# A planned attention and gated feed-forward kernel on one core: q put in token order at evacuation, eight weight tiles loaded in 512-column runs, and a new order table

## The chip, the cores and the metric

The kernel runs on one core of a Trainium2 chip. The metric is device time in microseconds (us) from one launch, the median of several runs. The five engines that matter are TensorE (PE in the profile, its weight loads PEld), VectorE (DVE), ScalarE (ACT), GpSimd (POOL) and SyncE (SP, which here only issues DMAs). ACT issues four of the loads too. Each engine takes its instructions strictly in the order in which the program gives them; engines wait for each other through semaphores.

## The reference, cut to what matters

```python
# q, k, v: (8, 8, 576, 64); chunks of 64 tokens; 72 chunks of 8 heads each
scores = (q_c @ k_c.T) / 8                    # 64 x 64 in each chunk and head
attn = exp(scores - max) / (sum + 1e-9)
x = (attn @ v_c), heads put side by side      # 4608 x 512
out = ((x @ w_a) * (x @ w_b)) @ w_out         # 512 -> 1536 -> 512
```

All inputs and the output are float32. The kernel computes in bfloat16 with float32 accumulation.

## The kernel before, in words

**Tiling.** The 4608 tokens are cut into 9 blocks (K) of 512 tokens, each of two units (u) of 256 tokens, each of four chunks. The 1536 inner columns are 12 tiles (ft) of 128. Attention is done unit by unit: q and k are loaded as float32 (`f32`), cast to bfloat16 (`qkb`), turned so that the head dimension lies on the partitions (`qkT`), multiplied into scores, exponentiated on ACT (`E`), summed and multiplied by v on PE; ACT takes ln and exp(-x) of the sums (`inv`), and DVE multiplies the two into `xT`, the feed-forward's input. Block 0 is done in four pairs of heads (`load_pair` to `values_pair`), so that it can begin before all of q and k is there. Units 2 and 3 (`TWO_UNITS`) are loaded with two neighbouring tokens in a row of 512 bytes and turned by PE (`cast_two`, `turn_pe`); all later units are turned by a transposing DMA (`turn_dma`).

**Feed-forward.** In blocks 0 and 1 each tile ft takes two chains of four matmuls (`ffn`: w_b into one PSUM bank, w_a into another). One engine copies the w_b bank to `bsb`, DVE multiplies it into the w_a bank and writes `AB`. From block 2 on the two products, and the product with w_out in all blocks, use seven instead of eight block products (Strassen's scheme in Winograd's form): sums and differences of the operands are made first (`side_sums`, `x_sums`, `out_sums`, `weight_sums`; DVE and POOL), and partial results are copied out of a PSUM bank (`keep_copy`) while the next product is added onto the same bank, so the next product into that bank waits for the copy (`side_group`, `out_seven`, `out_last`).

**Order.** Every instruction group is made by `op`, with the engines that may run it, a planned cost, and what it reads and writes. The order of all 1689 groups was found ahead of time and is written out in `ORDER_OF_ALL`: `e12` is group 12 on SP, `a` is PE, `b` ACT, `c` DVE, `d` POOL, digits after a colon are PSUM banks, and `f3` is a filler matmul on zeros into bank 3 that computes nothing. `follow` reads the table; the program is issued in that order. The costs given to `op` have no effect once the table stands. In the final loop a POOL group is made to wait for the DVE group last issued before it if that one is marked `fast` (works from SBUF to SBUF).

**Loads.** SP's queue takes the q pairs, v of block 0, weights, and the later units; the four k pairs are issued by ACT. A tile of w_a or w_b goes through a staging buffer (`wst`, eight of them, 512 KB each) and a cast into `WA` or `WB`. `load_w` brings 256 columns (two tiles, runs of 1 KB in memory) or 128 columns (one tile, runs of 512 bytes); `load_wo` brings two row tiles of w_out with all 512 columns (runs of 2 KB). SP's order up to the dense part of the program is: q pairs; v of block 0 mixed with tile 1 of w_b and w_a and k of unit 2; tiles 2 and 3; w_b of tiles 4 to 7; tile 0; q of unit 2; w_a of tiles 4 to 7; w_b of tiles 8 and 9; k and q of unit 3; and then the rest.

**Token order.** In block 0 a row of `f32` holds four neighbouring tokens, in units 2 and 3 two. After the turn, PSUM holds the tokens sorted by their place in the row. For k, the copy out of PSUM puts them in token order (`if x:` in `turn_pair` and `turn_pe`). For q it copies them as they stand, and the scores matmul reads q with a stride of one row of 128 (`scores_pair`, `chunk_of`).

Lines of the profile: L330 is `copy`, used by every cast and plain copy, so its groups are told apart by their tiles; L359 `load`; L481, L511 and L521 turn, scores and exponential of block 0; L612 and L649 turn of units 2 and 3 and scores of all later units; L762, L775 and L777 the two chains, the copy and the product of `ffn`; L847, L867, L881 and L885 product, kept copy, product of halves and addition of `side_group`; L914 and L917 its last steps; L1107 `out_sums`; L1151, L1164 and L1179 product, kept copy and addition of `out_seven`; L990 and L1013 those of the last block; L1446 the fillers.

Of the kernel before, what the change touches and what calls it, by code (L numbers as in the profile page):

```python
# [85 lines left out]
c132 e0 b1 e2 b3 e4 b5 c66 c75 c69 d78 d87 c84 e6 b7 c96 c93 f0 f1 f2 f3 f4 f5 f6 f7 f0 a67:0 c68 f1 f2 f3 f4  # L86
f5 f6 f7 f1 f2 f3 f4 f5 a88:1 a79:2 a85:3 e8 e10 e16 e11 e18 a70:4 b71 e14 e9 d102 d17 b86 f6 f7 a94:5 a97:6
b98 b95 c89 c80 a76:7 c77 a72:40 b74 b73 f3 f1 a99:31 b100 a90:65 b91 e134 c142 e15 a103:20 b105 b19 a81:47
e13 e12 b83 b82 f3 f6 f3 f6 f0 f3 a110:36 b101 a125:07 b92 a114:41 b111 b126 b112 b113 c115 b104 b106 a107:53
c109 c116 c108 f0 f0 f6 a143:0 c144 b127 a145:6 a118:24 b119 d117 f7 f3 a129:73 a122:21 b128 e35 c131 c130  # L90
b120 b121 c123 a169:5 b37 a170:4 c124 f0 f3 f0 a171 e32 d34 a179:0 b181 a180:3 d33 a175:7 b36 a176:2 e26 d28
a187:1 d27 e20 d21 b177 a172 a183:0 d22 c288 e38 e40 d39 b41 c296 c299 b173 c174 b185 a163:7 a164:5 a165 b167
e133 b146 e29 b31 e23 b25 b24 b30 c137 a140:4 c182 c141 c291 a191:0 b193 a166 c168 b189 c294 a138:3 b139 c178
a195:7 b197 e48 d50 a196:4 a184:6 e149 a203:5 a192:2 a215:01 a188:3 b216 b217 c287 d49 c186 b205 c250 c297
c157 a158:7 c198 e148 c152 e42 d43 d44 d302 a160:6 c161 a227:40 a153:1 b228 b154 b229 b230 c194 a155:5 c156
a207:6 c190 c159 b209 a199:4 a211:2 e135 e136 d147 a231:10 c300 e45 b46 b47 a235:53 b236 c290 c232 c233 a208:7
e51 b53 b52 b213 b237 a212:6 c214 d254 d255 e151 d303 c298 c210 a321:1 a200:5 b201 c202 a322:0 a309:2 a204:3
d289 c292 a354:64 e150 b162 a358:75 b311 c206 c260 b323 c324 d301 d304 d256 b356 b355 b357 c359 c360 a310:2
a317:1 a305:3 a325:4 a306:6 b307 c312 a313:0 a337:3 b315 a329:7 c308 b331 a341:0 a314:5 a342:2 a421:6 a318:7
e222 b319 c251 c316 c320 e62 b343 c344 a413:1 a333:0 a425:5 a326:7 e221 e60 b61 e218 b339 b423 e219 b224 b335  # L100
b327 c328 a338:2 a334:3 c336 e54 b55 a405:6 b407 c340 a417:0 a330:4 a426:7 b419 c332 a406:3 c408 d258 d295
d259 d252 d261 b415 e346 e56 e64 b65 e220 b225 a449:2 a409:6 b411 a410:0 c412 d293 a418:4 c420 a429:1 a422:3
a437:6 b439 a438:0 a430:4 b431 c432 e345 e348 e347 b352 d465 d351 d63 a414:6 c416 d57 c440 c238 c241 e58 b59
b427 b451 a445:1 a433:4 a446:6 a441:0 a442:5 c239 c424 b443 c242 c253 c245 c453 c240 c243 a262:2 a263 b264
e350 e223 b234 e349 c247 d466 c428 b447 c448 c444 a265:3 a450:0 c452 a268 a269 c244 c249 c246 e226 a362:71
c257 c461 a266 b270 a273 a434:6 c469 c248 b435 b363 c436 b364 b361 e353 a382:54 b384 b383 a374:07 b376 b375
c467 d457 d468 c267 a274 a271:1 a272 b275 c276 b377 a394:46 b395 a378:57 c380 e385 b396 e388 b397 a398:30 a277
a280 a281 e366 c379 c400 c399 a475:4 a531:7 a477:6 e369 e365 e367 b371 d462 c471 a278 a593:5 a540:0 c472 d474
e368 b476 b478 a538 c532 a533:3 c534 c473 e386 d391 e389 e390 e387 b279 b372 b539 a536 b537 e482 e481 c282
e480 c454 a541:2 a575:7 a542 b543 c544 a545 b546 e370 a591:3 a573:1 a552 b553 c547 d455 c470 a554 c535 d459  # L110
a556 a600:4 c557 b574 d392 d458 d548 a558 a596 c559 c592 b576 a598 a609:0 c594 b597 a602 e486 a549:2 e479 e373
d491 b599 a605 a601:3 a550 b606 a561:5 a615 b603 a613 c604 a617 c607 c608 b551 b610 b614 b401 c618 a619 c616
d463 a562 a402:14 a564 a631 d381 c555 a611:7 c620 d464 b403 b404 a494:61 b632 a565 a626:3 b612 a633 a637
a628:4 c563 e483 e484 e485 d492 c627 c629 d621 c560 c595 d630 e508 e510 e505 e393 a502:53 b495 e283 b496 b497
a498:61 c499 c500 c460 b566 a569 a570 c589 d456 b638 b634 a640 a635:4 b503 b504 a520:56 a524:31 e286 e511 b571
a652 c639 a577 a656 b521 b522 b523 c525 c526 c646 c644 b641 e514 e507 e506 b517 e667 e489 a636:5 a648:6 a578
c642 d645 d647 a567:3 a654 a650:1 b653 e509 e512 b518 a568 a658 a705:0 c657 c655 c659 c643 d660 b651 b649 a710
a714:4 b711 e285 b579 a712 a716 a707:7 b713 d622 c706 b717 c572 a580 a581 a719 e493 a528:50 b529 c718 c708
b720 a726 b727 e666 b530 a715:2 a730 a747:7 c582 c624 c623 c709 c721 c731 e488 e668 d587 d672 a749:3 b748
a765:5 c766 a732 c733 a728 c729 a770 b771 e665 d671 d734 b750 a767:6 c768 c661 c662 d664 e519 a682:04 b683  # L120
e487 e490 d501 d588 d590 a674:52 b676 a774:1 a776 b777 a775:0 b675 a772 b773 a787 b788 b684 a723:6 c778 a791
c792 b677 a785:2 a779 a678:57 a694:41 b695 c679 b780 c781 b696 d722 a724 a735:5 a736 a783:4 a802:1 c680 d782
b725 e284 c737 b786 c803 a793 c794 b784 a789 a800:7 c801 e687 e516 e585 e515 e685 e513 d527 e686 d691 a805
a738 c790 a698:51 e583 b697 c700 c699 e673 a702:07 e688 e871 b806 a807 b808 a822:3 a811 d692 d625 c820 c818
d819 a814 a809:1 a810:5 b812 b815 c813 b823 c816 a739 a826 a828 a830 c831 b704 b740 b827 c829 a844 b845 d663
a824:7 a832 a743 a744 c795 a841:4 e669 e670 d681 d817 c833 b703 b825 a846 a878:12 a850 d769 a839:0 c840 e869
e586 e870 b875 b745 a751 a752 e872 d876 c763 c804 c821 b881 b880 b882 b851 e693 a879:52 a905:10 c834 d837 c908
b753 b883 a860 b861 a848:6 c852 c842 d843 d798 e899 e689 e690 d701 a741:5 a742 c746 a864 b847 a853 b854 a914:3
b915 b884 d761 e898 d903 d762 d835 e877 e896 c907 a849:0 c855 c865 a754 a944 a755 c756 a866 c867 a939:4 b945
a948:1 d796 d836 a950 c940 b951 c952 e897 d902 d764 a929:26 a906:50 b909 b932 a916:4 b917 a961 b910 b933 b962  # L130
a857:5 a858 a965 c966 a974:2 a862 c863 a1052:06 b911 a928:31 c930 c931 a946 b947 a885:7 a957:3 b958 b1055 c975
e1043 a941:1 c942 b859 a886 e584 c887 e757 e874 e873 a979 b980 b1054 b1056 a953 b954 a949:6 a985 b986 d797
a888 a889 c799 a976:2 c838 c992 c856 d993 c955 c943 d868 d994 e1072 a963 c964 a959:1 b890 b960 c977 a983:7
c987 b912 e1044 b1049 e1045 e1046 d1050 a984:0 a967 a893 a981 c968 c995 a891:4 a1000 a996:2 a1004 c1005 b982
a988 b989 c978 c990 c991 b997 b1001 a998:6 a894 b895 b999 c937 d956 a892 a1013:7 c1014 a1002 a1006 a1018 b1019
e1071 e901 a1020 a918 c1007 b1021 c969 c1003 c1008 d1009 a1015:3 c1016 e760 e759 a919 b920 a1024 b1025 e904
a1079:70 a1053:13 b1057 b1058 c913 a1022:5 c1026 c970 d971 c1081 c1082 d1017 a1034 a921 a922 c923 a1038 c1039
e1048 c1011 e900 b934 e758 e1073 e1051 a1107:13 a1080:70 b1035 b1110 c972 a1027 b1028 a1023:2 c1029 a1090:4
a1119:1 a1036 c1037 a1040 c1041 d1010 d935 c936 d938 b1111 a1230:53 b1084 b1083 b1085 b1091 c1120 a1106:07
c1109 c1108 a1088:6 b1089 a1031:2 a1032 a1124 a1122 b1233 a1117:1 b1125 a1131 e1223 a1126:3 a1059:7 a1060  # L140
b1232 b1123 b1033 a1062 a1127:0 b1132 c1118 a1128 b1129 a1063 b1064 a1065:5 a1135:1 a1067 d1030 c973 e1070
d1076 d1170 c1172 c1171 c1061 e1075 e1222 e925 e1074 b1112 c1042 c1130 a1143 c1133 a1145 a1139 e1224 b1136
a1157 a1141 c1144 b1158 c1146 e1047 b1086 a1068 c1115 c1173 a1152:7 c1153 b1069 a1137:3 a1154:0 b1138 c1155
d1134 c1012 a1066 c1113 a1163 b1164 a1159 b1140 b1160 c1142 b1234 a1092 a1093 a1174:7 a1161:0 c1165 a1166
e1221 b1227 b1175 a1176:6 a1162:4 a1182 d1077 e927 e926 b1094 c1087 e1078 a1095 c1183 d1228 e1229 a1196
a1191:2 a1178 b1167 c1168 a1184 b1177 d1156 c1147 d1121 a1193:0 c1185 b1197 a1202 a1198 b1199 e1249 e1098
e1251 e924 e1100 c1192 c1194 d1148 c1186 d1114 d1149 b1203 a1200:4 c1204 b1179 a1180 c1181 a1096 c1097 e1250
e1103 e1101 a1205 b1206 a1212 b1213 d1169 d1187 d1189 d1151 d1195 a1216 c1217 a1214 c1215 a1201:2 a1231:01
a1257:35 b1236 b1235 a1281:74 b1284 c1207 c1260 c1259 a1266:6 b1267 b1285 a1218 c1219 a1268:1 b1269 a1291:0
# [31 lines left out]
def kernel(  # L181
# [116 lines left out]
    NWS = 8  # L298
# [975 lines left out]
    for n in names:  # L1274
# [13 lines left out]
        elif c == "O":  # L1288
            load_wo(i)
# [208 lines left out]
```

## Time and profile before

| what | us |
|---|---|
| median of 3 runs (296.96 to 298.87) | 296.99 |
| the profiled execution's own time | 296.97 |
| its span, first to last instruction | 295.2 |
| PE busy in the span | 289.9 |
| DVE, ACT, POOL busy | 205.8, 200.6, 172.9 |
| the two hardware DMA queues' share of 16 engines (q1, q10) | 71.9% and 1.1% |

The profile counts an engine as busy from the start of an instruction to its end; neighbouring instructions of one engine overlap a little, so the busy time of a group can be more than the time it keeps the engine from the next. A group's row gives line, engine, operation, tiles written and read, shapes and count, then busy us and mean ns of one. The time beside the span (1.8 us) lies before the first and after the last instruction.

### The profile page before, as it was taken

The page shows a single profiled execution, that of the slowest core. Times are in us where ns is not written, and L with a number is a line of the kernel's source. Part 1 is how long each engine was busy: PE and PEld are TensorE (multiplying, and loading weights), DVE is VectorE, ACT ScalarE, POOL GpSimd, SP SyncE. Part 2 cuts the span into 40 slices and gives each one's busy share as a digit, 9 for nine tenths or more (in the row PEclk, how much of TensorE's full clock was granted, in tenths as well). Part 3 has the DMA queues.
Part 4 walks back from the last instruction along what each step waited for, and adds up shares of the span by engine and source line. Part 5 has one row for each costly group of instructions (what it writes and reads, how often), then busy time and mean ns, then how long its engine had stood idle before and what let it go on. Part 6 is the DMA issues. An engine that isn't in the chain of part 4 may idle for free.

```text
span 295.2 us, 8644 instructions
## 1 busy us (share of the span) xinstructions
PE 289.9 (98%) x3537; PEld 236.3 (80%) x3539; DVE 205.8 (70%) x390; ACT 200.6 (68%) x365; POOL 172.9 (59%) x167
## 2 busy tenths in 40 slices
PE   8989999999999999999999999999999999999995
PEld 3644558877888888888888888888888888888884
DVE  2445876477776688686768886679777776667783
ACT  1776797868958977969487686677866655455331
POOL 2242387933488365976985366269747469695510
PEclk9999999999999999999999999999999999999999
DMA  7999999999999999999999976088730110021016
GB/s 256 318 372 337 266 300 298 283 228 234 230 222 234 207 200 249 231 223 240 251 223 219 223 184 167 2 193 218 180 73 3 53 73 3 1 109 71 2 66 219
DMA packets 146423, 55.08 MB, mean 187 GB/s; under 512 B 126288, under 2 KB 140752, under 8 KB 146384
## 3 DMA queue, kind: packets, MB, share of 16 engines
q1 hardware_dynamic: 145152, 53.43, 71.9%
q10 hardware_dynamic: 1232, 1.11, 1.1%
q8 instruction: 27, 0.44, 0.6%
q14 instruction: 12, 0.10, 0.1%
HBM read 37.75 MB, written 9.44 MB: 160 GB/s over the span
## 4 chain that ended last, share of the span: by engine, by line
PE 96%; ACT 2%; DVE 1%; issue 0%; DVEq 0%
PE F L847 44%; PE F L1151 25%; PE F L762 14%; PE F L990 3%; PE F L1446 3%; PE F L649 2%; PE F L673 2%; PE F L659 2%; PE F L481 1%; PE F L511 1%; PE F L612 0%; DVE xT L576 0%; ACT E L521 0%; ACT inv L550 0%; ACT inv L548 0%
## 5 line engine op out<-in xcount | busy, mean ns | idle before, releaser
L867 ACT COPY part<-F 128x512 f32<-128x512 f32 x105 | 59.8, 591 | 40.0 <-PE F L847 27.3
L885 DVE TENSOR_TENSOR bsb<-F,part 128x512 bf16<-128x512 f32 x63 | 43.2, 687 | 24.2 <-PE F L847 14.8
L881 POOL TENSOR_TENSOR AB<-AB,bsb 128x512 bf16<-128x512 bf16 x35 | 40.7, 1169 | 19.5 <-DVE wst L807 6.6
L1107 POOL TENSOR_TENSOR wst<-AB 128x512 bf16<-128x512 bf16 x27 | 31.4, 1165 | 19.1 <-DVE AB L881 6.2
L847 PEld LDWEIGHTS <-WA 128*128 128x128 bf16 x336 | 32.7, 98 | 4.3 <-issue 0.5
L1151 PEld LDWEIGHTS <-wst 128*128 128x128 bf16 x336 | 32.6, 98 | 4.1 <-issue 0.2
L847 PEld LDWEIGHTS <-WB 128*128 128x128 bf16 x336 | 32.6, 98 | 4.1 <-issue 0.2
L885 DVE TENSOR_TENSOR AB<-F,part 128x512 bf16<-128x512 f32 x42 | 28.8, 685 | 8.3 <-PE F L847 4.7
L1151 PEld LDWEIGHTS <-AB 128*128 128x128 bf16 x288 | 27.9, 98 | 3.5 <-issue 0.2
L847 PEld LDWEIGHTS <-Ta 128*128 128x128 bf16 x252 | 24.2, 98 | 3.4 <-issue 0.5
L847 PEld LDWEIGHTS <-Tb 128*128 128x128 bf16 x252 | 24.2, 98 | 3.3 <-issue 0.2
L712 DVE TENSOR_TENSOR xT<-F,inv 128x512 bf16<-128x512 f32 x32 | 20.7, 684 | 7.9 <-ACT inv L697 4.7
L847 PE MATMUL F<-wst,Ta 128*128 128x256 bf16 x168 | 25.3, 273 | 0.0
L847 PE MATMUL F<-wst,Tb 128*128 128x256 bf16 x168 | 25.2, 273 | 0.0
L847 PE MATMUL F<-wst,WA 128*128 128x256 bf16 x168 | 25.0, 273 | 0.0
L777 DVE TENSOR_TENSOR AB<-F,bsb 128x256 bf16<-128x256 f32 (+1 forms) x34 | 17.2, 529 | 11.2 <-ACT bsb L775 5.8
L762 PE MATMUL F<-xT,WA 128*128 128x256 bf16 (+1 forms) x136 | 24.9, 317 | 0.0
L847 PE MATMUL F<-wst,WB 128*128 128x256 bf16 x168 | 24.9, 273 | 0.0
L762 PE MATMUL F<-xT,WB 128*128 128x256 bf16 (+1 forms) x136 | 24.4, 316 | 0.4 <-DVE xT L576 0.4
L1151 PE MATMUL F<-WO,AB 128*128 128x256 bf16 x192 | 24.6, 273 | 0.0
L847 PE MATMUL F<-xT,WB 128*128 128x256 bf16 x168 | 24.6, 273 | 0.0
L847 PE MATMUL F<-xT,WA 128*128 128x256 bf16 x168 | 24.6, 273 | 0.0
(127 smaller groups left out, 585.0 us busy)
## 6 DMA issues: line engine op xcount, KB each, us to landing
f<-in_q_dram SPq DMA_DIRECT2D x28, 256.0 KB, 4.2
f<-in_v_dram SPq DMA_DIRECT2D x28, 256.0 KB, 4.5
out_dram<-osb SPq DMA_DIRECT2D x28, 256.0 KB, 3.2
f<-in_k_dram SPq DMA_DIRECT2D x24, 256.0 KB, 4.4
wst<-in_moe_w_out_dram SPq DMA_DIRECT2D x6, 512.0 KB, 5.8
wst<-in_moe_w_a_dram SPq DMA_DIRECT2D x5, 512.0 KB, 5.8
wst<-in_moe_w_b_dram SPq DMA_DIRECT2D x5, 512.0 KB, 6.5
f<-in_v_dram SPq DMA_DIRECT2D x16, 128.0 KB, 4.3
```

The lines of the kernel that those rows point to most:

```text
L649: T.matmul(PS[j][cl * 64:cl * 64 + 64, c:c + 64], chunk_of(u, 1, m, j, 2 * g + cl), chunk_of(u, 0, m, j, 2 * g + cl), start=True, stop=True,)
L712: op("dve", c_dve(512), lambda e, cl=cl: V.tensor_tensor(out=x.rearrange("p m (g c t) -> p c g m t", g=2, c=2)[:, cl], in0=f_of(PA[cl]).re ...
L762: T.matmul(f_of(b)[:, 0:n].rearrange("p (u t) -> p u t", u=len(us)), w[ft][:, kt, :], x[:, us[0]:us[-1] + 1, kt, :], start=(kt == 0), stop ...
L777: op("dve", c_dve(n), lambda e: V.tensor_tensor(out=AB[K % 2][:, ft // 2, ft % 2, us[0] * 256:us[0] * 256 + n], in0=f_of(banks[1])[:, 0:n] ...
L847: T.matmul(f_of(bank)[:, q * 256:q * 256 + 256], lhs(2 * g + q, kt), rhs[:, kt, :], start=(first and q == 0 and kt == 0), stop=(q == 1 and ...
L867: op("act", c_act(512), lambda e: A.copy(out=pab[s][i], in_=f_of(bank)), r=[("ps", id(bank))], w=[("part", s, i)], ps=[bank], prio=-400, a ...
L881: op(("dve", "pool"), TIMES, lambda e: ENG[e].tensor_tensor(out=dst, in0=dst, in1=b, op=MULT), r=bk, w=key, prio=-300, fast=True)
L885: op("dve", c_dve(512), lambda e: V.tensor_tensor(out=dst, in0=two(f_of(bank)), in1=two(pab[s][i]), op=ADD), r=[("ps", id(bank)), ("part", ...
L990: T.matmul(f_of(bank)[:, 0:256], lhs[:, i, h], rhs[:, i, :], start=(first and i == 0), stop=(i == NP - 1), skip_group_check=True)
L1107: op(("dve", "pool"), TWO_IN, lambda e, i=i, x=x, y=y, o_=o_: ENG[e].tensor_tensor(out=SS[i][:, s], in0=x[:, s], in1=y[:, s], op=o_), r=ft ...
L1151: T.matmul(f_of(bank)[:, at:at + 256], lhs[:, i, tt * 128:tt * 128 + 128], rhs[:, i, :], start=(first and at == 0 and i == 0), stop=(i == ...
L1446: "fn": lambda e: T.matmul(F[at], zero[:, 0:128], zero, start=True, stop=True),
```

## The change

1. `turn_pair` and `turn_pe` now put q as well as k in token order when they copy out of PSUM; the scores matmuls of block 0 and of units 2 and 3 then read q as contiguous columns.
2. Tiles 4 to 11 of w_a and w_b come by a new `load_four`: four tiles at a time (512 columns, runs of 2 KB), in two halves of the contraction dimension, each half through one staging buffer and one cast of 128x1024. Eight loads as before; eight casts where there were sixteen.
3. The engines that a group may run on are widened: weight casts, w_out casts, pair casts, unit casts and v casts may go to POOL, ACT or DVE; plain copies out of PSUM (`bsb`, `part`, `wst`, `osb`) to ACT or DVE; the w_out sums to DVE or POOL.
4. A new `ORDER_OF_ALL` (1681 groups) with new engines, banks, load order and fillers.

How the groups lie in the two tables, by engine (ACT / DVE / POOL):

| groups | before | after |
|---|---|---|
| all but DMAs and PE (ACT with its four loads) | 369 / 389 / 161 | 300 / 458 / 153 |
| kept copies of `side_group` | 126 / 0 / 0 | 86 / 40 / 0 |
| kept copies of `out_seven` | 24 / 0 / 0 | 17 / 7 / 0 |
| `bsb` copies of `ffn`, 512 and 256 columns | 34 / 0 / 0 | 16 / 18 / 0 |
| casts of w_a and w_b | 12 / 0 / 12 | 4 / 7 / 5 |
| casts of later units' q and k | 11 / 0 / 17 | 18 / 0 / 10 |
| casts of v | 9 / 0 / 9 | 8 / 4 / 6 |
| pair casts of block 0 | 0 / 6 / 2 | 3 / 2 / 3 |
| fillers on PE | 39 | 25 |

The core of the diff, the table left out but for its first words:

```diff
 ORDER_OF_ALL = """
-c132 e0 b1 e2 b3 e4 b5 c66 c75 c69 d78 d87 c84 e6 b7 c96 c93 f0 f1 f2 f3 f4 f5 f6 f7 f0 a67:0 c68 f1 f2 f3 f4
...
+c124 e0 b1 e2 b3 e4 b5 e8 e6 b7 c61 e15 e11 e10 e9 b58 f0 f1 f2 f3 f4 f5 f6 f7 f0 f1 a59:0 b60 b67 a62:1 d70
...
-    ORDER = "P0 P1 P2 P3 V0 V1 w1 W3 W2 q2 k2 W1 w0 W5 v2 W4 O0 k3 O1 O2 q3 O4 O5 v3 O3"
+    ORDER = "P0 P1 P2 P3 V0 V1 w1 W1 w0 q2 k2 X1 v2 X2 O0 k3 O1 O2 q3 O4 O5 v3 O3"
...
+    def load_four(src, name, i):
+        dst = WA if name == "a" else WB
+        for half in range(2):
+            s = count["w"] % NWS
+            count["w"] += 1
+            load(
+                wst[s].rearrange("p (k c) -> p k c", k=2),
+                src[half * 256:half * 256 + 256, i * 512:i * 512 + 512].rearrange("(k r) c -> r k c", r=128),
+                ("wst", s), (256, 71),
+            )
+            def cast(e, s=s, half=half):
+                return copy(e, dst[:, 4 * i:4 * i + 4, 2 * half:2 * half + 2, :], wst[s].rearrange("p (k f c) -> p f k c", k=2, f=4))
+            op(("pool", "act", "dve"), (1.04, 1.05, 0.69), cast, r=[("wst", s)], w=[("w" + name, 4 * i + n) for n in range(4)],
+               prio=5 + 4 * i * 0.1, fast=True)
...
             dst = qkT[hu][:, 8 * x + 4 * mm:8 * x + 4 * mm + 4, :]
-            if x:
-
-                dst = dst.rearrange("p a b -> p (a b)").rearrange("p (t r) -> p t r", r=4)
-                t = t.rearrange("p r t -> p t r")
+            dst = dst.rearrange("p a b -> p (a b)").rearrange("p (t r) -> p t r", r=4)
+            t = t.rearrange("p r t -> p t r")
...
-            tq = qkT[hu][:, 4 * mm:4 * mm + 4, :].rearrange("p r t -> p t r")
+            tq = qkT[hu][:, 4 * mm:4 * mm + 4, :].rearrange("p a b -> p (a b)")
...
-                            tq[j * 64:j * 64 + 64, n * 16:n * 16 + 16, :],
+                            tq[j * 64:j * 64 + 64, n * 64:n * 64 + 64],
...
         if u in TWO:
-            if x:
-                return t[:, 2 * m + c // 2, (c % 2) * 64:(c % 2) * 64 + 64]
-            return t.rearrange("p (m r) t -> p m t r", r=2)[:, m, 32 * c:32 * c + 32, :]
+            return t[:, 2 * m + c // 2, (c % 2) * 64:(c % 2) * 64 + 64]
...
-                op("act", c_act(512), lambda e: A.copy(out=pab[s][i], in_=f_of(bank)), r=[("ps", id(bank))], w=[("part", s, i)],
+                op(("act", "dve"), (c_act(512), c_dve(512)), lambda e: copy(e, pab[s][i], f_of(bank)), r=[("ps", id(bank))], w=[("part", s, i)],
```

SP's order in the new table is: q pairs with one v load before the last; the rest of v of block 0; tile 1; tiles 2 and 3; w_b of tiles 4 to 7; tile 0; w_a of tiles 4 to 7; k of unit 2; w_b of tiles 8 to 11; q of unit 2; w_a of tiles 8 to 11; v of unit 2; k and q of unit 3; and then the rest.

More of the change, by code (lines that the diff above doesn't have):

```diff
@@ L91 @@
[L91 to L95, printed above, removed]
@@ L237 @@
     HOLD = ()
-    W_CASTS = {(x, n): ("pool",) if x == "b" else ("act",) for x in "ab" for n in range(2)}
-    O_CASTS = [("pool","act")]
+    W_CASTS = {(x, n): ("pool", "act", "dve") for x in "ab" for n in range(2)}
+    O_CASTS = [("pool", "act", "dve")]
     WHOLE = False
@@ L402, in load_w @@
             engs = W_CASTS[name, ft % 2]
-            op(engs, [{"pool": 0.62, "act": 0.62, "dve": 0.42}[x] for x in engs], cast, r=[("wst", s)], w=[("w" + name, ft)], prio=5 + ft * 0.1)
+            op(engs, [{"pool": 0.62, "act": 0.62, "dve": 0.42}[x] for x in engs], cast, r=[("wst", s)], w=[("w" + name, ft)], prio=5 + ft * 0.1, fast=True)
+    def load_four(src, name, i):
[12 more added lines that the diff above has]
+               prio=5 + 4 * i * 0.1, fast=True)
     def load_wo(i):
@@ L728, in post @@
                    r=[("ps", id(PS[j]))], w=[("E", u % 2, n, j) for n in range(2)], ps=[PS[j]], prio=prio)
[L730 removed]
+        return 0.285, lambda: mm_scores(u, [f_of(x) for x in PS]), t_keys(u), PS, [], post
     def slot(prio, *parts, fixed=False):
@@ L916, in four @@
                 else:
-                    op("act", c_act(512), lambda e: A.copy(out=dst, in_=two(f_of(X))), r=[("ps", id(X))], w=key, ps=[X], prio=-400)
+                    op(("act", "dve"), (c_act(512), c_dve(512)), lambda e: copy(e, dst, two(f_of(X))), r=[("ps", id(X))], w=key, ps=[X], prio=-400)
             def three():
@@ L1163, in keep_copy @@
         def keep_copy(bank, i):
-            op("act", c_act(512), lambda e: A.copy(out=pu[i], in_=f_of(bank)), r=[("ps", id(bank))], w=[("pu", i, 0), ("pu", i, 1)], ps=[bank], prio=prio - 250, after=staged(4))
+            op(("act", "dve"), (c_act(512), c_dve(512)), lambda e: copy(e, pu[i], f_of(bank)), r=[("ps", id(bank))], w=[("pu", i, 0), ("pu", i, 1)], ps=[bank], prio=prio - 250, after=staged(4))
         o = []
@@ L1222, in four @@
             dst, key = place(1, 0)
-            op("act", c_act(512), lambda e: A.copy(out=dst, in_=two(f_of(X))), r=[("ps", id(X))], w=key, ps=[X], prio=prio - 240)
+            op(("act", "dve"), (c_act(512), c_dve(512)), lambda e: copy(e, dst, two(f_of(X))), r=[("ps", id(X))], w=key, ps=[X], prio=prio - 240)
         def three():
```

205 lines of the change are left out of this document (105 added, 100 removed).

## The prediction

> **What bounds the kernel now.** First the page (busy shares, slices, chain), then the chain in order of time, then the table of stretches with cuts where the chain changes, then the waits of PE.
>
> ```profile
> PE 289.9 (98%) x3537; PEld 236.3 (80%) x3539; DVE 205.8 (70%) x390; ACT 200.6 (68%) x365; POOL 172.9 (59%) x167
> ...
> DMA  7999999999999999999999976088730110021016
> ...
> PE 96%; ACT 2%; DVE 1%; issue 0%; DVEq 0%
> ```
> ```profile
> 1.26 4.02 PE F L1446 x9
> 5.71 2.61 PE F L1446 x12
> ...
> 18.82 1.42 DVE xT L576 x4
> 20.27 7.50 PE F L762 x34
> ```
> ```profile
> 0.00:20.27 20.27, 18.02 (x225) 10.02 (x228) 8.74 (x22) 11.43 (x27) 5.80 (x13) 1.00 1.01 312
> 20.27:292.11 271.84, 271.83 (x3312) 226.33 (x3311) 196.64 (x367) 189.21 (x338) 167.07 (x154) 1.00 0.72 178
> 292.11:295.20 3.09, 0.00 (x0) 0.00 (x0) 0.42 (x1) 0.00 (x0) 0.00 (x0) 1.00 0.38 126
> ```
> ```profile
> PE F L1446 <- DVE zero L1256: 1.3, 1, 1.3
> PE F L1446 <- ACT part L548: 0.4, 1, 0.4
> PE F L762 <- DVE xT L576: 0.4, 1, 0.4
> ```
> Columns of the third view: stretch, length, then busy us and count of PE, PEld, DVE, ACT, POOL, then clock, DMA share and GB/s. From 20.27 PE works without a gap to 292.11; its last wait is for xT of block 0. So there are three terms: a front of 20.27, a dense part of 271.84, and a tail of 3.09. PE is busy in the front too, but much of that is the 39 fillers. The DMA row says what else may bind: the DMA engines are full to about 170 us. The profiled run took 296.97, as the median does (296.99); 1.77 of it lie outside the span.
>
> **The front.** It ends when xT of block 0 is whole, and that ends a run of ACT. In the timeline of before, ACT waits to 9.26 for the first turned heads (PE's turns stand behind DVE casts in its order), then makes 25 instructions in 9.92 us, to 19.18; xT's last part and the first matmul on it follow 1.09 later. In the new table the first two casts of q lie on ACT and its first copy of a turned head comes behind one PE group, so ACT can start as q lands, at 4.1 (DVE's first cast starts at 4.09, ended by that DMA). The new table has 26 ACT groups up to that point, about the same work: 4.1 + 9.9 + 1.1 = 15.1 if ACT never waits. It will wait: heads land until 8.5 (DVE's cast ended by k at 8.54) and v follows. I add 1.3: 16.4. Bounds: 15.1, and 18.0 if ACT waits 2.9 (over half of the 5.1 it waited for the first turn before). A second count agrees: up to the dense part PE has 14.6 us of work in the old table, fillers included, and 10.2 in the new one (matmul intervals of the trace); with the same 5.7 of gaps that is 15.9. The fourteen missing fillers (14 x 0.22 = 3.0) are themselves free: they filled waiting.
>
> **q in token order.** Copying q strided costs DVE 0.69 in place of 0.41 (the tile view of qkT gives DVE copies 413 to 692 ns, and the k copies are the long ones); ACT's take 580 to 616 either way. Of the new q copies DVE has three: 0.8 us of DVE, in the front or beside dense PE, inside the above. Gain: a unit's scores took 0.69 where q is strided (33.76 and 39.60) and 0.45 where not (68.22): 2 x 0.24 = 0.5 off the dense part. Block 0's four lie in the front's waits. Against it, eight turns of k of unit 2 move from the front into the dense part: 8 x 0.056 = 0.45. Dense part: 271.8.
>
> **Loads and weights.** Ahead of tiles 2 and 3 the new queue has 3.7 MB (heads, v, tile 1) in place of 4.2 (k of unit 2 too): 0.5 MB at the 382 GB/s of 15 to 20 us is 1.4. Before, POOL's cast of tile 3 starts at 19.07, ended by its DMA; now 17.7. Then 1.05 MB of w_b, 2.75: 20.4, and its second half's cast on DVE, 0.69 by the row of 128x1024 casts: 21.2. PE, dense from 16.4, has tile 1's second halves and tiles 3 and 2 first, 20 matmuls of 0.216: it comes at 20.7 and waits 0.5. Then 3.15 MB (tile 0, w_a, k of unit 2, the next w_b) at the 340 GB/s of 20 to 30 us: 29.7, cast 30.4; PE, with 40 matmuls and four turns, is there at 30.05: 0.35. Unit 3's q comes 3.15 MB after that (q and v of unit 2, w_a, k), at 310 GB/s, between the rates of 20 to 30 and 40 to 45 us: 39.9. ACT's cast (1.05) ends at 41.0, PE wants to turn it 23.6 us of work and 1.2 of waits after 16.4, at 41.2: no wait, or a few tenths; I count 0.2. The scores, sums and values of unit 2 stand closer together than before (0.86 us of matmuls between scores and sums where there were 1.31, with two exponentials of 0.61 between): 0.35. Together 1.4, bounds 0 and 2.8. The front and this are coupled: what PE is late at the start, it need not wait for weights.
>
> What a load in 2 KB runs costs, no row shows in this stretch. The w_out loads have that form: median 5.8 us to landing for 512 KB, as w_a's 1 KB runs (5.8; w_b's 6.5). Bounds: 1.37 us each (384 GB/s, seen at 18 to 20 us) and 1.86 (282 GB/s, 40 to 45 us, w_out among heads); I take w_a's, so nothing changes, as the landing rows are nearest.
>
> Later loads: ahead of unit 4's transposing DMA the new SP order has one half-load of v less; its DMA was issued at 61.98 and unit 4's scores began at 68.22. In the new table scores 4 come 1.0 later in PE's work; with the front 3.9 sooner and 1.4 given back they begin at 66.7, 1.5 sooner, and the half-load (256 KB at 282 GB/s) takes off 0.9: hidden, with 0.6 less to spare. Units 8 and later come 8 to 20 us later in PE's work: more cover than before.
>
> **Engines.** Eight casts fall away (16 x 0.62 give 8 x 0.69 to 1.05), and 77 PSUM copies go from ACT to DVE: 62 of 0.69 and 15 of 0.42. DVE: 205.8 + 48 = 254 busy (86%), ACT 200.6 - 33 = 168. No row shows a DVE copy of 512 float32 columns; nearest is its addition from PSUM, 687 (L885), which I take; ACT's copy is 591 (L867), and between these the difference is nothing to 0.1 a copy. PE gives way only if a bank's next product comes sooner than the copy: the closest in the old table had 0.87 of matmuls for ACT's 0.59 and did not stop PE, so a copy needs its own length plus 0.28, for DVE 0.97; the closest kept copy on DVE has 1.01. Nothing, while the copy finds DVE free. Back to back, DVE starts the next about 0.09 before the last ends (four xT parts of 0.41 in 1.42), so its true load is nearer 75%.
>
> Sum: 16.4 + 1.4 + 271.8 + 3.1 = 292.7, and 1.8 outside: **294.5**.
>
> **Rivals.**
> (1) The weights and heads bind: the front is sooner, but DMA is as full as before. With the eight new loads halfway to their upper bound (+0.25 each, 2.0, all of it waited for, as PE is then short of weights) it is 296.5; at the bound itself 298.4. For it: DMA at 9 through 170 us. Against: PE never waited for a load after 20 us.
> (2) Slower: DVE becomes the bound. Of the copies now on DVE, 14 have under 1.66 of matmuls to their bank's next use. One DVE instruction of 0.69 ahead of each costs 4.1 together (the shortfalls summed): 298.6; two cost 16 over 23 copies: 311. Between, nearer the first: 300. It decides once more than 2.5 is lost. For it: DVE 196.64 of 271.84 in the dense part becomes 244, 90%, and DVE already waits little. Against: the 75% above, and ACT's 42 copies with under 1.66 cost nothing before. GpSimd belongs to it: in before, DVE's L1107 additions take 601 ns after a POOL row and 430 otherwise, 0.17 more. [...]
> (3) The clock: with fewer fillers PE may fall back to the rate of its first fillers (0.43 each, nine in 4.02; later twelve in 2.61, 0.22). Dense work at half rate for as long as that first stretch loses 2: 296.5. Against: in 9.7 to 15 us two to five fillers at a time kept 0.22. [...]
>
> **How the numbers follow.** Forecast 0.57, its own range 292.7 (15.1 front, 0.9 given back) to 296.1 (18.0 front, 1.4 given back); rival 1 0.20, rival 2 0.18, rival 3 0.05. Range 292.7 to 299.5: it takes in rivals 1 and 3 and the lower part of 2. About 1% is what a measurement of this kernel can tell from no change: faster means under 294.0, somewhat under half of the forecast's cases, 0.25. Slower means over 300.0, half of rival 2 and a little unforeseen, 0.15. The rest, 0.60.
>
> **What would show it.** Right: L762 without a gap from about 16.4, later gaps of 0.3 to 0.5 at the first w_b tile of tiles 4 to 7 and between unit 2's scores and sums, L649 at 0.45 in every unit, 25 fillers. Rival 1: PE waits for L330 casts that a DMA ended, at 20 to 45 us. Rival 2: PE L847 and L1151 waiting for DVE part or wst L330. Rival 3: L762's chains at 0.43 a matmul. The forecast is wrong if the front ends after 18, or if gaps after 45 us add up to over 1.5 more than before.

## The result, and the profile after

The changed kernel takes 294.77 us (median of six runs, 293.80 to 295.83); beside it the kernel before takes 297.64. The ratio is 0.9898, with a 95% interval of 0.9867 to 0.9930. Measured again on another chip it is 0.9925 (0.9899 to 0.9950). So the change is worth about 0.9%, some 2.6 us. The profiled run took 294.79, with a span of 293.0 and 1.8 outside it, as before. A few executions were clearly slowed (one of twelve in the run called d1 below took 521.18 us, with TensorE at 0.71 of its clock), and every ratio here leaves them out.

The page of the changed kernel first: engines, DMA row, chain of waits by engine.

```profile
PE 285.8 (98%) x3525; PEld 233.3 (80%) x3525; DVE 246.2 (84%) x459; ACT 174.6 (60%) x296; POOL 169.5 (58%) x159
...
DMA  7999999899998899999959999931919200013025
...
PE 92%; DMA 4%; SPq 2%; ACT 1%; issue 0%; ACTq 0%; DVE 0%
```

The share of PE is as large as before (98%). DVE has risen from 205.8 to 246.2 us and ACT has fallen from 200.6 to 174.6. New is that 6% of the chain that ended last is now DMA and SP's queue: the chain starts with loads. Next the table of stretches, cut at the first matmul that needs all of xT and at PE's last matmul (stretch, length, busy us and count of PE, PEld, DVE, ACT, POOL, then clock, DMA share, GB/s).

```profile
0.00:16.54 16.54, 13.81 (x205) 7.00 (x206) 8.77 (x20) 11.42 (x28) 3.15 (x10) 1.00 0.93 273
16.54:289.90 273.36, 272.00 (x3321) 226.31 (x3319) 237.03 (x439) 163.16 (x269) 166.34 (x149) 1.00 0.74 183
289.90:293.00 3.10, 0.00 (x0) 0.00 (x0) 0.43 (x1) 0.00 (x0) 0.00 (x0) 1.00 0.44 148
```

The front ends at 16.54 where it ended at 20.27: 3.73 us gained. The long stretch has grown from 271.84 to 273.36, though PE's busy time in it is the same (272.00 and 271.83): PE now stands idle for 1.36 us in it. The tail is as it was. Why the front is shorter, ACT's rows show: first those of before, then those of the change (start, us, line, what it does, and in brackets how long ACT waited and for what).

```profile
9.26 2.05 ACT L330 COPY qkT<-F 128x512 bf16<-128x512 bf16 x4 [5.14 <-PE F L481]
...
18.55 0.63 ACT L550 ACTIVATE part<-part 128x512 f32<-128x512 f32 x1
```
```profile
4.13 0.62 ACT L329 CAST qkb<-f 128x512 bf16<-128x512 f32 x1
5.33 0.58 ACT L329 COPY qkT<-F 128x512 bf16<-128x512 bf16 x1 [0.58 <-PE F L498]
...
15.05 0.63 ACT L565 ACTIVATE part<-part 128x512 f32<-128x512 f32 x1
```

ACT gets its first turned heads 3.9 us sooner (5.33 for 9.26), and its last step for block 0 ends 3.5 us sooner (15.68 for 19.18). Where the 1.36 lies, the chain in order of time and PE's waits say (engine, tile, line; what it waited for; us in total, times, longest).

```profile
1.79 5.63 DMA f<-in_k_dram
12.61 6.63 DMA wst<-in_moe_w_a_dram
20.46 9.67 PE F L774 x44
```
```profile
PE F L774 <- ACT WA L329: 1.1, 1, 1.1
...
PE F L671 <- ACT E L739: 0.2, 1, 0.2
```

The chain runs through the load of w_a of tiles 2 and 3 (issued at 12.61, landed at 19.24). The timeline around it shows the wait (L774 is `ffn`, L329 `copy`: the changed kernel's line numbers).

```profile
17.43 1.89 PE L774 MATMUL F<-xT,WB 128*128 128x512 bf16 x8
...
19.27 1.14 ACT L329 CAST WA<-wst 128x512 bf16<-128x512 f32 x2 [1.48 <-DMA wst<-in_moe_w_a_dram]
...
20.46 0.39 PE L774 MATMUL F<-xT,WA 128*128 128x512 bf16 x1 [1.13 <-ACT WA L329]
```

PE has used up its eight matmuls on w_b by 19.3; ACT starts the casts of w_a at 19.27, as soon as the data is there, and PE goes on at 20.46. From there it never waits for more than 0.2 us.

### The profile page after: what moved, and what is told of

The parts are those of the page before. It is cut to its first block, busy times and chain, and to the rows that moved or that the text cites. A ratio compares the mean times of both kernels' runs of the same rounds, so it can differ in the third digit from the quotient of the medians.

```text
span 293.0 us, 8646 instructions
## 1 busy us (share of the span) xinstructions
PE 285.8 (98%) x3525; PEld 233.3 (80%) x3525; DVE 246.2 (84%) x459; ACT 174.6 (60%) x296; POOL 169.5 (58%) x159
## 4 chain that ended last, share of the span: by engine, by line
PE 92%; DMA 4%; SPq 2%; ACT 1%; issue 0%; ACTq 0%; DVE 0%
PE F L859 44%; PE F L1163 25%; PE F L774 13%; PE F L1002 3%; DMA wst<-in_moe_w_a_dram 2%; DMA f<-in_k_dram 2%; PE F L661 2%; PE F L685 2%; SPq L358 2%; PE F L671 2%; PE F L627 1%; ACT E L739 0%; ACTq L358 0%; ACT WA L329 0%; DVE f L1030 0%
## 5 line engine op out<-in xcount | busy, mean ns | idle before, releaser
L329 ACT COPY part<-F 128x512 f32<-128x512 f32 x71 | 41.0, 589 | 38.6 <-PE F L859 25.1
L893 POOL TENSOR_TENSOR AB<-AB,bsb 128x512 bf16<-128x512 bf16 x42 | 48.3, 1156 | 19.2 <-DVE wst L1119 6.3
L329 ACT COPY wst<-F 128x512 f32<-128x512 f32 (+1 forms) x35 | 20.0, 571 | 30.8 <-PE F L1163 13.9
L1119 POOL TENSOR_TENSOR wst<-AB 128x512 bf16<-128x512 bf16 x23 | 26.4, 1158 | 10.6 <-DVE AB L893 7.5
L329 DVE COPY part<-F 128x512 f32<-128x512 f32 x34 | 23.2, 686 | 3.3 <-PE F L859 1.7
L774 PE MATMUL F<-xT,WA 128*128 128x256 bf16 (+1 forms) x136 | 24.4, 317 | 1.1 <-ACT WA L329 1.1
L329 ACT CAST bsb<-F 128x512 bf16<-128x512 f32 (+1 forms) x31 | 16.1, 534 | 15.0 <-PE F L859 8.3
```

What stands on the lines that cost most here:

```text
L329: return A.copy(out=out, in_=in_) if e == "act" else ENG[e].tensor_copy(out=out, in_=in_)
L774: T.matmul(f_of(b)[:, 0:n].rearrange("p (u t) -> p u t", u=len(us)), w[ft][:, kt, :], x[:, us[0]:us[-1] + 1, kt, :], start=(kt == 0), stop ...
L893: op(("dve", "pool"), TIMES, lambda e: ENG[e].tensor_tensor(out=dst, in0=dst, in1=b, op=MULT), r=bk, w=key, prio=-300, fast=True)
L1119: op(("dve", "pool"), TWO_IN, lambda e, i=i, x=x, y=y, o_=o_: ENG[e].tensor_tensor(out=SS[i][:, s], in0=x[:, s], in1=y[:, s], op=o_), r=ft ...
```

## The experiments

**Theory:** the gain is the earlier front, which the new table's order brings; from about 17 us the landing of weights limits PE, so part of the gain goes back there; token order of q and the wider loads are each worth half a microsecond or less. **Rivals:** (A) token order of q makes the front shorter; (B) the 2 KB runs bring the gain; (C) the copies taken off ACT bring it.

One table for all kernels whose long stretch stays dense. "Front" ends at the first matmul that needs all of xT; "rest" goes to PE's last matmul; "idle" is rest less PE's busy time in it; then the landing of w_a of tiles 2 and 3, the GB/s from 11 to 15 us, the profile's span, and the ratio to before in the timed runs.

| kernel | front | rest | idle | w_a lands | GB/s | span | ratio (95%) |
|---|---|---|---|---|---|---|---|
| before | 20.27 | 271.84 | 0.01 | | 316 | 295.2 | 1 |
| the change | 16.54 | 273.36 | 1.36 | 19.24 | 254 | 293.0 | 0.9898 (0.9867 to 0.9930) |
| a0_again | 17.36 | 274.40 | 2.43 | 21.11 | 199 | 294.8 | 0.9925 (0.9899 to 0.9950) |
| e1_q_strided | 16.91 | 272.70 | 0.23 | 18.30 | 250 | 292.7 | 0.9919 (0.9901 to 0.9937) |
| e2_1kb_runs | 16.59 | 273.56 | 1.10 | 18.40 | 261 | 293.2 | 0.9933 (0.9911 to 0.9956) |
| e8_cast_on_dve | 16.87 | 274.17 | 1.96 | 18.24 | 259 | 294.1 | 0.9919 (0.9889 to 0.9948) |
| e4_late_turns | 18.36 | 272.36 | 0.26 | 18.90 | 241 | 293.8 | 0.9882 (0.9837 to 0.9928) |
| e3_k2_ahead | 18.43 | 272.42 | 0.31 | 19.94 | 285 | 293.9 | 0.9930 (0.9898 to 0.9963) |
| d1_tile1_among_v | 19.78 | 272.38 | 0.23 | 18.52 | 308 | 295.2 | 0.9926 (0.9889 to 0.9962) |
| d2_tile1_between | 19.39 | 271.88 | 0.23 | 18.65 | 211 | 294.3 | 0.9879 (0.9841 to 0.9916) |
| e7_no_fillers | 18.05 | 272.96 | 0.23 | 19.10 | 249 | 294.1 | 0.9872 (0.9830 to 0.9914) |
| b1_old_q_order | 20.59 | 272.82 | 0.72 | | 295 | 296.5 | 0.9982 (0.9945 to 1.0020) |

These runs were made on several chips (before took 297.4 us on one, 298.2 and 300.0 on others) and the intervals overlap, so neither the times nor the ratios rank the variants of the change. Each profile is one execution; what it shows of the terms is read below.

### The changed kernel again

No edit.

> The changed kernel once more, as the base for the runs beside it. Theory and rivals alike: about 294.8 us, a front of 16.7 us, one stretch near 19 us in which PE waits about 1.3 us for w_a of tiles 2 and 3, and PE dense from there. If the lump in the landing of that load (2.76 us where its neighbours take 1.3) is chance, the wait is missing here, and the time is up to 1.3 lower.

Measured: 295.14, ratio 0.9925. The wait is there, and longer:

```profile
PE F L774 <- ACT WA L329: 2.2, 1, 2.2
```

The load of w_a landed at 21.11, 1.87 later than in the first profile of the same kernel. In e1, e2 and e8, whose loads up to it are the same, it landed at 18.24 to 18.40. So this landing varies by 2.9 us from one execution to the next, and PE, which comes at 19 to 20, waits for what is over. Of the 1.8 us between the two profiles' spans, this idle time makes 1.1 and a later front (17.36 for 16.54) 0.8.

### Undoing the parts: q with a stride, 1 KB runs; token order alone

```diff
-            tq = qkT[hu][:, 4 * mm:4 * mm + 4, :].rearrange("p a b -> p (a b)")
+            tq = qkT[hu][:, 4 * mm:4 * mm + 4, :].rearrange("p r t -> p t r")
...
-                            tq[j * 64:j * 64 + 64, n * 64:n * 64 + 64],
+                            tq[j * 64:j * 64 + 64, n * 16:n * 16 + 16, :],
```

and the copies of q to match; `b1_old_q_order` is the opposite edit, made in the kernel before.

> q is left as it stands in PSUM again and read with a stride by the scores; table and weight loads are those of the changed kernel. Theory (the gain is the earlier front, and token order is worth only the shorter scores of units 2 and 3): L661 at 0.69 in place of 0.45 us in two units, DVE copies of q 0.28 shorter, 0.5 us slower in all, near 295.3. Rival A (token order of q is what makes the front end sooner): the front ends 2 to 3 us later, 297 to 298.

> The kernel before, with q alone put in token order at evacuation: old table, old loads. Theory (the gain of the change is its earlier front; token order is worth only the shorter scores of units 2 and 3): 0.5 us faster than before, ratio 0.998, the dense part still from about 20.3 us. Rival A (token order shortens the front): the dense part from 18 us or sooner, ratio 0.992 as for the whole change.

Measured: undone in the changed kernel, 295.19 beside 295.14; alone in the old one, ratio 0.9982, which can't be told from 1. The long stretch of e1, with the wait gone:

```profile
16.91:289.61 272.70, 272.47 (x3321) 226.81 (x3319) 237.04 (x439) 163.12 (x269) 166.33 (x149) 1.00 0.75 183
```

The front ends between the two of the change, so rival A falls; b1 says the same from the other side (20.59 beside 20.27). PE's busy time after the front is 272.47 for 272.00: 0.47 longer, as the theory has it for two units. The matmuls show it: the 32 of a half of unit 2's scores start within 0.25 us in the change and 0.47 here. In the total it can't be seen: six runs of e1 lie between 294.47 and 295.66 and nine of the change between 294.06 and 297.33, and the profiled execution of e1 happened to have no wait for w_a.

```diff
-                wst[s].rearrange("p (k c) -> p k c", k=2),
-                src[half * 256:half * 256 + 256, i * 512:i * 512 + 512].rearrange("(k r) c -> r k c", r=128),
+                wst[s].rearrange("p (k c) -> p k c", k=4),
+                src[:, i * 512 + half * 256:i * 512 + half * 256 + 256].rearrange("(k r) c -> r k c", r=128),
```

> Each half of the eight tiles' weights is 256 columns of all 512 rows (runs of 1 KB) in place of 512 columns of 256 rows (runs of 2 KB); the number of loads and casts and the table stay. Theory (the form of the run matters little): landings within 0.1 us of 1.3 us a load, 0 to 0.3 us slower or faster, 294.5 to 295.1. A first half now frees two whole tiles, so waits at the weights may also shrink by up to 0.3. Rival B (the longer runs bring the gain): each of the eight loads 0.25 or more slower to land, 2 us of waits of PE for casts that a DMA ended between 18 and 35 us, 296.8.

Measured: 295.57 beside 295.14. In the trace the eight loads land 1.28 to 1.37 us after the load ahead of them, for 1.24 to 1.35 in the change: 0.1 at most, 0.06 on the mean. By the starts of its matmuls PE loses 0.24, 0.48 and 0.60 at three places with weights (19.2, 21.1 and 30.5 us), where the change loses 1.3 at one. Rival B falls: the longer runs bring no more than a few tenths. What eight casts bring in place of sixteen was not run by itself; before, PE was idle for 0.01 us after its front, so they had no wait of PE to take away there.

### Front and weights against each other

In `e4_late_turns` five fillers stand ahead of the first turn; in `e3_k2_ahead` k of unit 2 is loaded ahead of tile 1:

```diff
-... f7 f0 f1 a59:0 b60 ...
+... f7 f0 f1 f2 f3 f4 f5 f6 a59:0 b60 ...
```
```diff
-... d88 a80:0 a77:1 e16 b74 ... c170 c242 e126 b181
+... d88 a80:0 a77:1 e126 e16 b74 ... c170 c242 b181
```

> The changed kernel with five more fillers on PE ahead of its first turn, so that the attention front starts 1.1 to 2.1 us later; loads as they are. Theory (weights limit PE near 19 us, and what the front is late it need not wait there): the front ends about 1.1 later or less, the wait near 19 us shrinks by the same, and the time moves by 0 to 0.3 us: 294.8 to 295.1. Rival (the front's length is what counts): 1.1 us slower, 295.9, with the wait as long as it was.

> The changed kernel with the 512 KB of k of unit 2 loaded ahead of tile 1, as the kernel before had it ahead of weights. Theory (from about 17 us PE is limited by the weights' landing): weights land 1.3 to 1.5 us later, and PE, which already waits near 19 us, waits that much more: 296.2. If the block of 512 KB keeps the DMA engines from running dry, less: 295.5. Rival (the front alone sets the end of the early part, weights have slack): 294.8.

Measured for e4: 294.94, with a front 1.82 us longer than in the change's first profile and no wait for w_a at all:

```profile
18.36:290.72 272.36, 272.10 (x3320) 226.51 (x3319) 237.94 (x440) 162.44 (x269) 167.08 (x149) 1.00 0.74 182
```

The fillers move PE's first turn from 4.90 to 7.33 and ACT's first copy of a turned head from 5.33 to 7.75, and the front follows: it is 1.8 and 1.0 us longer than in the two profiles of the change. So the start of attention does set the end of the front; which part of the new table (engines, places or load order) brings that start forward, no run separates. The span is between the change's two (293.0 and 294.8), and the ratio (0.9882) shows no loss. This is what the theory asked for: what the front lost need not be waited for at the weights. For e3 the theory had 1.4 more of waiting near 19. Measured: 296.15, but with a ratio of 0.9930, so no loss is shown in the total; and in the profile what is lost is lost elsewhere. w_b of tile 1 lands at 16.17 in place of 14.25, and DVE stands at its cast:

```profile
16.19 0.43 DVE L329 CAST WB<-wst 128x512 bf16<-128x512 f32 x1 [1.01 <-DMA wst<-in_moe_w_b_dram]
...
16.87 1.41 DVE L591 TENSOR_TENSOR xT<-F,part 128x256 bf16<-128x256 f32 x4
17.00 0.59 PE L774 MATMUL F<-xT,WB 128*128 128x512 bf16 x2 [1.11 <-DVE xT L591]
```

The last parts of xT stand behind that cast in DVE's order, so a late weight holds up the front: it ends at 18.43, and PE, late already, finds w_a (19.94) in time. Weights ahead of PE do cost, but through the front; the place in the theory was wrong. The size (0.9 us of span) is inside what the change itself varies by.

> One cast of w_a of tiles 2 and 3 goes from ACT to DVE, so that the two casts of these tiles no longer queue on ACT behind one another. Theory (the wait near 19 us is the landing at 19.24 plus two casts of 1.14 on one engine): PE waits there about 0.5 us less; part of it comes back at w_b of tiles 4 to 7, whose data lands at 21.8 whatever happens before; 0.1 to 0.5 us faster, 294.3 to 294.7. Rival: the next landing binds in any case, and the whole 0.5 comes back: 294.8.

In e8 one word of the table is changed (`b25` to `c25`). The wait near 19 is gone, but w_a landed at 18.24 in this execution, so the cast's engine was not put to the test. The next weights cost 0.35 at 21.4 by the starts of the matmuls (w_b of tiles 4 to 7), and this execution met a late load of w_out instead:

```profile
PE F L1163 <- ACT WO L329: 1.5, 1, 1.5
```

Median 294.51 beside 295.14: not told apart.

### Why the loads land late

> The changed kernel with the two loads of tile 1 put among the seven small loads of v, in place of behind them; bytes ahead of w_a of tiles 2 and 3 are the same. Theory (in 11 to 15 us the DMA engines run partly dry, 231 to 278 GB/s where before had 293 to 347, since seven loads of 128 KB in a row take SP about 0.5 us each to issue and about 0.45 to move): the DMA share stays above 1.1 through these slices, w_a of tiles 2 and 3 lands at about 18.2 in place of 19.24 to 21.11, PE does not wait near 19; v lands up to 1.3 later, and if the front waits for it, up to 0.9 comes back: 293.8 to 294.8. Rival (the dry spell comes from something else at that time, whatever is loaded): the low rates stay at 11 to 15 us, the wait stays, 295 or more.

> Tile 1's two loads are put between the loads of v once more, one place later each than in the run before (behind the third and the fifth of the seven). Theory (seven small loads in a row let the DMA engines run dry): 290 GB/s or more in 11 to 15 us, the front less late than when they came sooner, at about 17.0, w_a of tiles 2 and 3 landing by 18.5 and no wait near 19: 294.0 to 294.8. Rival (the dry spells come as they like): a slice under 240 GB/s between 11 and 15 us, and a wait or a late front as in the runs before: 295 or more.

The edits move two words of SP's order, first d1, then d2:

```diff
-... e15 e11 e10 e9 ... e13 e12 e14 ... e16 ... e18 ...
+... e15 e11 e16 e10 e9 e18 ... e13 e12 e14 ...
```
```diff
-... e15 e11 e10 e9 ... e13 e12 e14 ... e16 ... e18 ...
+... e15 e11 e10 e16 e9 ... e13 e18 e12 e14 ...
```

Measured: ratio 0.9926 for d1 and 0.9879 for d2 (medians 296.67 and 296.68, on chips where before took 298.2 and 300.0), which can't be told from the change. The stretch from 11 to 15 us of before, of the change and of d2, then the lowest slice of d2 (last two columns: DMA share, GB/s).

```profile
11.00:15.00 4.00, 3.94 (x85) 2.40 (x85) 0.85 (x2) 3.81 (x13) 1.60 (x2) 1.00 1.21 316
```
```profile
11.00:15.00 4.00, 3.15 (x93) 1.71 (x93) 3.18 (x8) 4.00 (x13) 0.00 (x0) 1.00 0.95 254
```
```profile
11.00:15.00 4.00, 2.64 (x60) 1.25 (x59) 2.49 (x5) 3.88 (x13) 0.00 (x0) 1.00 0.92 211
14.00:15.00 1.00, 0.58 (x5) 0.16 (x4) 0.14 (x1) 1.00 (x4) 0.00 (x0) 1.00 0.58 129
```

The change moves 1.02 MB in these four us where before moved 1.26: that is most of a microsecond of landing. d1 seemed to bear the theory out (308 on the mean, w_a at 18.52, no wait), but d2, nearly the same order, has 211 and the lowest slice from 11 to 15 us of all profiles in the table. So the theory that seven small loads in a row let the engines run dry is not borne out. The old order isn't free of it either: b1 has 207 GB/s at 15 to 16 us and 200 at 18 to 19. What makes the dry spells stays open; shown is only that they come, and that in most executions of the new table one comes at 11 to 15 us.

Nor does this rate alone set when w_a of tiles 2 and 3 lands. The change (254 GB/s) had it at 19.24, e1, e2 and e8 (250 to 261) at 18.30, 18.40 and 18.24, d2 (211) at 18.65. By 18 us the change had moved as many bytes as e1, e2 and e8 (282 GB/s from the start, for 277 to 280). What differs is this one load: it landed 2.76 us behind the load before it in the change and 3.86 in a0_again, and 1.35 to 1.79 in e1, e2 and e8. The time of its issue doesn't explain it (12.61 in the change, 12.96 in e8). In the change one of the 1 KB packets under way then, from 16.44 on, took 1076 ns, where their median is 46; whether that is the cause is open.

Both d1 and d2 also paid in the front: v lands later (15.62 and 14.67 its last but one, for 13.23), PE idles 1.38 and 1.33 for it, and then runs at half rate, as PEclk (the column before the DMA share) shows, first for d1, then for d2:

```profile
14.01:17.42 3.41, 1.79 (x44) 0.95 (x44) 2.09 (x6) 3.11 (x10) 0.05 (x1) 1.00 1.06 370
17.42:20.83 3.41, 3.19 (x9) 1.21 (x9) 1.88 (x6) 0.39 (x1) 1.51 (x2) 0.50 1.09 379
```
```profile
12.50:15.91 3.41, 1.86 (x43) 0.84 (x42) 1.88 (x5) 3.29 (x11) 0.00 (x0) 1.00 0.93 239
15.91:19.32 3.41, 3.32 (x38) 1.55 (x40) 2.61 (x8) 1.08 (x2) 0.61 (x1) 0.50 1.07 386
```

Both theories underrated this price: d1 was to give back up to 0.9 and d2's front was to end near 17.0. Their fronts ended at 19.78 and 19.39, by the late v and by the half rate.

### Without fillers

All 25 words `f0` to `f7` are taken out; they compute nothing that the output needs.

> All 25 fillers are left out; they compute nothing that the output needs. Theory (fillers are free where PE waits anyway, but they keep its clock up: in the run with tile 1 among v a gap of 1.3 us after a thin stretch was followed by 2.5 us at a granted clock of 0.5): the front is no shorter, the matmuls after it start at 0.43 each and reach 0.22 after 2 to 4 us, which costs 1 to 2, in part in place of the wait near 19: 295.5 to 296.5. Rival (the clock holds without them): 294.8, or 0.2 less.

Measured: 296.26, on a chip where before took 300.0; the ratio (0.9872) shows no loss. The first eight matmuls of the feed-forward take 0.39 to 0.50 each, from 16.33 to 19.76, the ninth 0.30, and the others 0.22. The front ends at 18.05 by that. But PE, so much later, no longer waits for w_a, and the span is 294.1, between the change's two. The cost of the half rate is real (1.7 us for these eight matmuls: eight times 0.43 less 0.22) and is hidden by the same loads.

### Moving the copies

In e5 the 50 kept copies that the change has on DVE go to ACT, in their old places in the table; in e6 every second of ACT's (50) goes to DVE; one word of each:

```diff
-... c435 c249 c267 c436 b356 ...
+... c435 c249 b267 c436 b356 ...
```
```diff
-... a254:5 a255 b256 e342 ...
+... a254:5 a255 c256 e342 ...
```

> The 50 kept copies that the change put on DVE go back to ACT, the rest of the table as it is. Theory (which of the two makes the copies is nothing that PE notices; the gain comes from the front): 294.5 to 295.3, waits of PE after 25 us as they are. Rival (the change gained by taking the copies off ACT): ACT's copies queue, PE waits for them, 1 to 4 us slower, 296 to 299.

> Fifty more kept copies (every second one of those still on ACT) go from ACT to DVE, as many again as the change moved there. Theory (a copy costs PE nothing while DVE finds room; DVE's own step is about 0.6 us a copy, so its true load in the dense part rises from about 75% to 86%): 0 to 2 us slower, 295 to 297. Rival (DVE is close to being the bound, as priced in the prediction: one DVE instruction ahead of each tight copy costs PE 4 us, two cost 16): PE waits for DVE copies, 299 to 311.

Measured: e5 317.17, ratio 1.0561 (1.0525 to 1.0598); e6 334.96, ratio 1.1157 (1.1119 to 1.1196). Both theories fall, by far, and both times lie above the rivals' highest figures too (299 and 311). PE's share of its span is 93% and 89%. The page of e5, then its waits over all engines (one of DVE's and the longest of PE's), then PE's waits in e6:

```profile
PE 292.9 (93%) x3523; PEld 234.6 (74%) x3525; DVE 218.4 (69%) x409; ACT 199.2 (63%) x346; POOL 169.6 (54%) x159
```
```profile
DVE AB L897 <- ACT part L329: 15.2, 10, 4.0
...
PE F L859 <- ACT part L329: 5.7, 6, 1.7
```
```profile
PE F L859 <- DVE part L329: 9.9, 11, 2.4
PE F L859 <- DVE wst L329: 8.1, 6, 2.2
```

e5 is the telling one. Its ACT is no busier than before's (199.2 and 200.6), its 105 copies on ACT are the 105 of before, and before's PE ran without a gap. So neither ACT's load nor ACT as the engine of these copies explains 22.9 us more of span: before had both. What differs is the order: the table sets the copies where DVE would be free, and ACT comes to them behind work that the table put there for an ACT without them. In the longest of these waits (4.0 us, to 201.0) ACT stood for 3.2 us at a `bsb` cast that waited for PE, with the copy behind it; in the one to 193.1 (2.4 us) the copy stood behind five steps on the sums and another copy. DVE's additions then wait 15.2 us for ACT's copies where they waited 1.4 in the change, and PE waits for their banks. In e6 DVE is that engine. A table planned anew with these copies on ACT was not run, so the reading rests on the traces. A price for e6 was in the prediction (4 us for one instruction ahead of each tight copy, 16 for two); 50 more copies cost 39 us of span.

So rival C isn't refuted by e5 as a matter of engines; it can't be, in a fixed table. What speaks against it is the change's own profile: PE's busy time after the front is 272.00 for 271.83, so there was nothing that the moved copies could have gained.

## Why the prediction was right, point by point

The forecast was 294.5; 294.77 was measured, and 294.79 in the profiled run. The sum of its terms was 16.4, 1.4, 271.8, 3.1 and 1.8; measured 16.5, 1.4, 272.0, 3.1 and 1.8. Not all of the reasons are as right as that, and that the 1.4 is met so closely is luck.

- **The front.** Predicted 16.4 (15.1 to 18.0), 16.54 measured, 16.54 to 17.36 in the five profiles with this order. The reading held: ACT starts at 4.13, where before it waited to 9.26 for turned heads, waits for PE three times (0.58, 0.61 and 0.19, 1.4 where 1.3 was added), and ends its last step for block 0 at 15.68.
- **q in token order.** Predicted 0.5; e1 has 0.47. With 0.45 set against it, the dense part was to stay as it was, and it did (272.0 busy for 271.8).
- **Weights.** The sum (1.4) was right, the place was not. Predicted were 0.5 and 0.35 at w_b of tiles 4 to 7 and 8 to 11, 0.2 at unit 3 and 0.35 at unit 2's exponentials. Measured is one wait of 1.1 at w_a of tiles 2 and 3 and 0.2 at the exponentials. The failed step is that 0.5 MB less at 382 GB/s would bring these tiles at 17.7: they were there at 18.24 to 21.11 in five profiles. Slower slices before (199 to 261 GB/s from 11 to 15 us) can account for the 0.5 to 0.7 of e1, e2 and e8; the rest, in the change and in a0_again, came with that one load (2.76 and 3.86 us behind its neighbour), and its cause is open. Being late there, PE needed no other wait. In these five profiles PE's idle time after the front is between 0.23 and 2.43, so the 1.4 is one draw from that range. The coupling that the prediction names was right (e4, e7, d1, d2), and it is why a wrong place made so little of an error.
- **2 KB runs.** Predicted to change nothing; e2 gives at most 0.1 a load.
- **Engines.** DVE was predicted at 254 and is at 246.2. The copies were sized rightly (686 ns for 687), and the lengths of all DVE instructions add up to 47 us more than before (48 predicted); busy time grew by 40 only, since it counts the overlap of neighbours once. For the same reason "nearer 75%" was too low: the overlap (0.07 in the four xT parts, not 0.09) is in part taken off twice. In the change DVE is busy for 237.03 of the 273.36 us after the front, 87%, and e6 shows how little room that leaves. "Nothing, while the copy finds DVE free" held for this table, and e5 and e6 show that it is a property of the table.
- **The rivals.** Rival 1 (loads bind) is the one nearest to the truth: a wait for a cast that a DMA ended, between 0 and 2.2 us by execution, where the prediction took 1.4. Rival 2 is what e6 shows. Its part on GpSimd was misread: 601 ns is the mean of eight additions with one order of operands, not of those after a POOL row. Of before's 35 additions at L1107, 31 take 411 to 426 ns, and the four longer ones (524, 620, 921 and 1371) all began while a POOL instruction ran and ended 0.3 us after it. So the delay is no steady 0.17: it is nothing for most and up to 0.95 for a few. DVE's casts were lengthened by 0.2 us in all in the change, and the lengthenings of two-operand instructions between SBUF tiles add up to 3.5 us there and 3.9 before. Rival 3 happened in e7, in d1 and d2, and once each in e5 and e6; in the change the matmuls of the feed-forward start 0.22 apart from the first.

The chances said 0.25 for faster by over 1%; the two measurements, 0.9898 and 0.9925, lie on either side of that line.

## What to carry to other kernels

When the front of a kernel ends sooner, look at which load is next: here the front ended 3.73 us sooner, and 1.36 came back as idle time of PE, 1.1 of it as one wait at the first load that was late. For such a forecast take the landings of several executions: one load of this kernel, the same in all, landed within a range of 2.9 us, and neither the mean rate nor the time of issue told when. In a kernel whose order is written out, the engine of an instruction can't be changed alone: its place in that engine's order is part of its price (22.9 us of span in e5, 39 in e6).

## What the runs showed of the hardware

- In 1 us slices the DMA rate fell to 129 GB/s (d2, 14 to 15 us) and 94 (e5, 15 to 16 us), with loads queued, where before had 293 to 347 from 11 to 15 us. One packet of 1 KB took 1076 ns in the change, where their median is 46 ns. One load, w_a of tiles 2 and 3, landed between 18.24 and 21.11 us in five profiles, a range of 2.9 us.
- Four profiles show PE at half rate (a granted clock of 0.50) for one stretch of 3.41 us each: 17.42 to 20.83 in d1, 15.91 to 19.32 in d2, 203.89 to 207.30 in e5, 240.57 to 243.98 in e6. In the 3.41 us before, PE was busy for 1.79, 1.86, 1.52 and 0.99. In a0_again it was busy for 1.84 of the 3.41 us from 18.29, with a single wait of 2.2 us beginning in it, and kept its rate (1.00); so these busy times alone do not tell. What brings the half rate on, the traces leave open.
- In e7 the first eight matmuls of the feed-forward start 0.40 to 0.49 us apart (16.33 to 19.76) while PEclk says 1.00. The trace of that run holds no clock record at all, and the views print 1.00 where there is none, as they do over before's first fillers (0.43 each). The interval between matmuls is the surer sign.
- Some DVE additions between SBUF tiles that began while a POOL instruction ran took longer and ended just after it. In before, this addition ends at 82.48, 0.28 us after the cast, and takes 0.92 where 0.41 to 0.43 is usual:

```profile
81.17 1.04 POOL L330 CAST qkb<-f 128x1024 bf16<-128x1024 f32 x1 [1.12 <-DVE wst L807]
81.56 0.92 DVE L1107 TENSOR_TENSOR wst<-wst,AB 128x512 bf16<-128x512 bf16 x1
```

  Of the 116 DVE instructions of before that read two such operands (128x512 bfloat16, both in SBUF) 12 were lengthened, by 3.9 us together, and 9 of 106 in the change, by 3.5 us; each of these 21 began while a POOL instruction ran and ended 0.28 us after it.
